# Reordering the start of a fused attention and long-convolution kernel: two head groups per key tile, taps spread by TensorE, x turned in the background, three load buffers

## The chip, the cores and the metric

The kernel runs on one core of a Trainium2 chip. The metric is device time in microseconds (us), the median of several runs. Engine names in the profile: PE is TensorE (PEld its weight loads), DVE is VectorE, ACT is ScalarE, POOL is GpSimd, SP is the engine whose queue issues most loads. A name such as L423 is a line of that kernel's source; a "q" behind an engine's name is its queue for issuing transfers.

## The reference, cut to what matters

```python
# A: attention, S=2048, D=512, 32 heads of 16
qkv = (x @ wqkv).reshape(B, S, 3, H, Dh).transpose(2, 0, 3, 1, 4)
p = softmax(einsum("bhqd,bhkd->bhqk", q, k) * Dh ** -0.5)
a = einsum("bhqk,bhkd->bhqd", p, v).transpose(...).reshape(B, S, D) @ wo
# B: 4-tap shift, then a causal convolution as long as the sequence
k_shift = sum_t k_pad[:, t:t + S, :] * shift_k[:, 3 - t]
kv = k_shift * v
y = irfft(rfft(kv, 2S) * rfft(ssm_k, 2S))[:S] + kv * ssm_D
b = q * y
out = concatenate([a, b], -1)
```

## The kernel before

The program records operations per engine, and each engine works its own list in order (the stop before 73.16 us, below, shows one list holding up another for 4.11 us). The main loop runs over *chunks*: a chunk is two or three blocks, and a block is one head's scores of 128 keys against 512 queries, one bank of PSUM (the array PS, to which every matmul of the traces writes; exp reads 128x1536 f32 from it for three blocks; copying a result out of a bank is called *evacuating* it). Four heads are a group. Per chunk TensorE makes the scores, ScalarE takes one exp over all the chunk's banks, and two chunks later TensorE multiplies by V ("PV"). The *taps* are the four factors per channel of the shift in B; the *pieces* (key pieces and convolution pieces are the same thing) are the VectorE operations that make kv from k, v and the taps. In between comes one *background* slot: first the projection units of Q, K and V (`early`), later the convolution on TensorE, with further Q projections and the output projection at its boundaries.

```python
def emit_qk(T):                     # scores of chunk T, then exp
    ... e.matmul(PS[:, bank, :], lhsT=KTo[...], rhs=QT[...], tile_position=(32 * s, 0))
    h_exp[T] = act.op(lambda e: e.activation(PT[:, T % R_PT, 0:n * QB], PS[:, banks...], ACT.Exp, scale=SCALE), ...)

# the taps: 512 KB broadcast load, then one ScalarE copy that transposes them
h_tb[0] = act.op(lambda e: e.activation(TB.rearrange("p m d -> p d m"), TRAW, ACT.Copy), [h_traw])

def kv_chunk(j):                    # 256 keys: 8 "pieces" on VectorE
    b = kvbuf[j % 2]                # two load buffers: k shifted by 0..3, and v
    ... 4 multiplies by a tap, 3 adds, then two multiplies by v; then load_kv(j + 2)

early = [("v", 0), ("v", 1), ("v", 2), ("k", 0, 1), ("v", 3), ...]   # units, one a chunk
def emit_bg(T):                     # the background slot of chunk T
    if st["early"] < len(early):
        unit(early[st["early"]], (5, 7)[T % 2] ...)   # 4 matmuls, then VectorE evacuates
        return
    if not kv_pieces and not st["started"]:
        st["started"] = True
        load_wop(...); load_wr(d) for 12 convolution rows; load_qn(...)
    ... turn / output projection / later q units / conv_lags(...)

for T in range(NT + 3):
    emit_qk(T)
    ... PV of chunk T-2 ...
    emit_bg(T)
    for _ in range(1 if T < 20 else 2):
        if kv_pieces and T >= 1:
            kv_pieces.pop(0)()      # convolution pieces on VectorE
```

The convolution needs every piece: its right-hand rows (`WR`, 512 KB each, loaded with a skew from a scratch tensor) reuse the load buffers' memory, so they are asked for only after the last piece. Cuts are marked by dots.

The softmax here doesn't subtract the row's maximum and nothing guards it: scores larger than these inputs give would overflow.

## Time and profile before

| | before |
|---|---|
| time | 1025.4 us median (1025.0 to 1025.6) |
| span of the profiled run | 1023.0 us |
| ScalarE busy | 948.8 us, of which exp 933.3 |
| first exp starts | 21.8 us |
| chunk 56 starts | 134.9 us |
| last exp ends | 1008.2 us |

The profile's page, kernel before. First the busy time of each engine, then two rows of the timeline in 40 slices (each digit is the busy share of a slice in tenths), then the chain that ended last, by engine:

```profile
PE 764.5 (75%) x12876; PEld 344.8 (34%) x12876; DVE 312.7 (31%) x478; ACT 948.8 (93%) x701; POOL 57.6 (6%) x82
...
DVE  3789413232203232321122423122222231222222
ACT  7766589999999999999999899999999999999994
...
ACT 78%; PE 9%; DVE 6%; DMA 5%; POOL 1%; SPq 1%; issue 0%; ACTq 0%; DVEq 0%
```

ScalarE is the bound: it is at 9 from the seventh slice on but for one 8 and the last slice, and 78% of the chain. The large losses are where its digits are below 9, above all in the first 140 us. Here is the ScalarE timeline of the first stretch (start, duration, engine, line, operation, out<-in, shapes, how many merged; in brackets the idle time before it and who ended that). L423 is exp:

```profile
13.01 9.30 ACT L377 ACTIVATE WR<-WR 128x2048 bf16<-128x2048 bf16 x1 [0.19 <-DMA WR<-in_B_shift_k_dram]
21.82 4.02 ACT L423 ACTIVATE PT<-PS 128x1536 bf16<-128x1536 f32 x3
...
45.47 1.45 ACT L423 ACTIVATE PT<-PS 128x1536 bf16<-128x1536 f32 x1 [0.60 <-PE PS L416]
47.08 1.02 ACT L423 ACTIVATE PT<-PS 128x1024 bf16<-128x1024 f32 x1 [0.16 <-PE PS L416]
...
73.16 2.54 ACT L423 ACTIVATE PT<-PS 128x1024 bf16<-128x1024 f32 x2 [5.63 <-PE PS L416]
...
124.28 5.81 ACT L423 ACTIVATE PT<-PS 128x1536 bf16<-128x1536 f32 x4 [9.35 <-PE PS L416]
134.86 26.65 ACT L423 ACTIVATE PT<-PS 128x1536 bf16<-128x1536 f32 x19 [4.77 <-PE PS L416]
```

Four things are to be seen. ScalarE transposes the taps for 9.30 us before the first exp. From 27 to 55 us the exps are apart: 45.47 to 47.08 is 1.61 us for a chunk, while the exps alone last 1.45 and 1.02. There is a stop of 5.63 us before 73.16. And there are stops of 9.35 and 4.77 us before 124.28 and 134.86. Counting exps one by one gives the number of the chunk: chunk 56 is the one at 134.86, and the remaining 636 chunks have three banks each, except the last.

The windows view of the same kernel, a line for each stretch (busy us of each engine with the number of instructions, then the granted TensorE clock, the share of the 16 DMA engines, and GB/s):

```profile
core 0: us, PE busy (x) PEld busy (x) DVE busy (x) ACT busy (x) POOL busy (x), PEclk, DMA share, GB/s
60.00:80.00 20.00, 14.41 (x68) 3.87 (x68) 17.66 (x32) 11.41 (x11) 4.05 (x7) 0.83 0.60 219
80.00:100.00 20.00, 12.74 (x74) 3.91 (x74) 18.57 (x32) 11.72 (x10) 10.80 (x15) 1.00 0.56 180
```

From 60 to 100 us VectorE is 88 to 93% busy, ScalarE under 60%. The stop of 5.63 us before 73.16 shows how one list holds up another (a line of VectorE's timeline and one of TensorE's):

```profile
68.80 0.69 DVE L325 TENSOR_TENSOR WR<-WR 128x1024 bf16<-128x1024 bf16 x1 [2.05 <-DMA WR<-in_B_v_dram]
70.14 0.62 PE L449 MATMUL PS<-PT,VAF 128*32 128x512 bf16 x4 [4.11 <-DVE OF L464]
```

VectorE waits 2.05 us for a load; the copy that frees the bank of the first group's PV (L464) stands behind that in its list, and TensorE waits 4.11 us for the copy. And in TensorE's timeline the first convolution matmul waits for its rows:

```profile
123.04 0.66 PE L560 MATMUL PS<-WR,KV 128*16 128x128 bf16 x16 [8.85 <-DMA WR<-kz_scratch]
```

### The profile page before, as it was taken

The page shows a single profiled execution, that of the slowest core. Times are in us where ns is not written, and L with a number is a line of the kernel's source. Part 1 is how long each engine was busy: PE and PEld are TensorE (multiplying, and loading weights), DVE is VectorE, ACT ScalarE, POOL GpSimd, SP SyncE. Part 2 cuts the span into 40 slices and gives each one's busy share as a digit, 9 for nine tenths or more (in the row PEclk, how much of TensorE's full clock was granted, in tenths as well). Part 3 has the DMA queues.
Part 4 walks back from the last instruction along what each step waited for, and adds up shares of the span by engine and source line. Part 5 has one row for each costly group of instructions (what it writes and reads, how often), then busy time and mean ns, then how long its engine had stood idle before and what let it go on. Part 6 is the DMA issues. An engine that isn't in the chain of part 4 may idle for free.

```text
span 1023.0 us, 27854 instructions
## 1 busy us (share of the span) xinstructions
PE 764.5 (75%) x12876; PEld 344.8 (34%) x12876; DVE 312.7 (31%) x478; ACT 948.8 (93%) x701; POOL 57.6 (6%) x82
## 2 busy tenths in 40 slices
PE   6986667776778777777676967776777786768887
PEld 2322233333333333333333333333333333331111
DVE  3789413232203232321122423122222231222222
ACT  7766589999999999999999899999999999999994
POOL 4124300000001000000000000000000000000000
PEclk8989789999999999999999999999999999995557
DMA  9254699899997798999999498999999959950000
GB/s 319 83 190 154 168 392 401 301 366 353 366 391 271 264 389 299 369 331 379 385 379 405 162 335 329 359 343 376 390 383 373 395 195 385 377 187 9 1 1 21
DMA packets 85124, 296.07 MB, mean 289 GB/s; under 512 B 10768, under 2 KB 14865, under 8 KB 84624
## 3 DMA queue, kind: packets, MB, share of 16 engines
q1 hardware_dynamic: 77760, 275.94, 71.8%
q0 software_dynamic: 5232, 16.78, 5.4%
q8 instruction: 101, 1.65, 0.6%
q10 hardware_dynamic: 2016, 1.57, 0.5%
q14 instruction: 15, 0.12, 0.0%
HBM read 287.83 MB, written 6.42 MB: 288 GB/s over the span
## 4 chain that ended last, share of the span: by engine, by line
ACT 78%; PE 9%; DVE 6%; DMA 5%; POOL 1%; SPq 1%; issue 0%; ACTq 0%; DVEq 0%
ACT PT L423 77%; PE PS L512 3%; DMA WR<-kz_scratch 2%; PE PS L268 2%; PE PS L416 2%; PE PS L282 1%; PE PS L449 1%; DMA WR<-in_B_v_dram 1%; DVE QT L296 1%; DMA WR<-in_B_shift_k_dram 1%; DVE WR L325 1%; ACT WR L377 1%; DVE WR L329 1%; DVE OUTA L520 1%; DVE DN L472 1%; POOL WR L148 1%
## 5 line engine op out<-in xcount | busy, mean ns | idle before, releaser
L423 ACT ACTIVATE PT<-PS 128x1536 bf16<-128x1536 f32 (+1 forms) x692 | 933.3, 1668 | 53.1 <-PE PS L416 52.7
L416 PE MATMUL PS<-QT,KTo 32*128 32x512 bf16 x2048 | 287.5, 409 | 211.0 <-ACT PT L423 209.3
L560 PE MATMUL PS<-WR,KV 128*16 128x128 bf16 (+15 forms) x8192 | 304.9, 223 | 20.0 <-DMA WR<-kz_scratch 16.2
L449 PE MATMUL PS<-PT,VAF 128*32 128x512 bf16 x2048 | 292.6, 414 | 4.1 <-DVE OF L464 4.1
L560 PEld LDWEIGHTS PS<-WR,KV 128*14 128x14 bf16 (+15 forms) x8192 | 204.6, 106 | 42.3 <-issue 26.7
L416 PEld LDWEIGHTS PS<-QT,KTo 32*128 32x128 bf16 x2048 | 67.8, 91 | 375.3 <-ACT PT L423 341.7
L449 PEld LDWEIGHTS PS<-PT,VAF 128*32 128x32 bf16 x2048 | 69.2, 94 | 177.1 <-issue 165.8
L464 DVE COPY OF<-PS 128x512 f32<-128x512 f32 x32 | 22.1, 692 | 341.4 <-PE PS L449 341.4
L472 DVE RECIPROCAL DN<-DN 128x128 f32<-128x128 f32 x128 | 110.7, 916 | 0.9
L576 DVE CAST YB<-PS 128x512 bf16<-128x512 f32 x32 | 22.1, 691 | 274.5 <-PE PS L560 274.4
L148 POOL DMA_DIRECT2D out_dram<-QN x4 | 4.7, 1171 | 622.9 <-DVE QN L596 622.9
L268 PE MATMUL PS<-xT,WQP 128*128 128x512 bf16 x128 | 34.0, 389 | 6.2 <-DVE KTo L300 3.2
L512 PE MATMUL PS<-WKV,OTN 128*128 128x512 bf16 x128 | 34.5, 399 | 3.6 <-DVE OTN L477 2.3
L148 POOL DMA_DIRECT2D WR<-in_B_k_dram x35 | 24.7, 710 | 63.7 <-DVE KV L334 54.5
L296 DVE CAST QT<-PS 128x512 bf16<-128x512 f32 x32 | 22.0, 689 | 20.1 <-PE PS L268 20.1
L466 DVE STREAM_SHUFFLE DN<-OF 128x512 f32<-128x512 f32 x32 | 24.9, 777 | 0.0
L477 DVE TENSOR_TENSOR OTN<-OF,DN 128x512 bf16<-128x512 f32 (+1 forms) x35 | 23.3, 667 | 1.0
L275 PE MATMUL PS<-xT,WKV 128*128 128x512 bf16 x64 | 18.5, 416 | 5.5 <-DVE KTo L300 4.4
L325 DVE TENSOR_TENSOR WR<-WR 128x1024 bf16<-128x1024 bf16 x32 | 21.5, 677 | 3.2 <-DMA WR<-in_B_v_dram 3.2
L282 PE MATMUL PS<-WKV,xT 128*128 128x512 bf16 x64 | 18.8, 422 | 0.0
L512 PEld LDWEIGHTS PS<-WKV,OTN 128*128 128x128 bf16 x128 | 10.8, 101 | 21.8 <-issue 6.0
L268 PEld LDWEIGHTS PS<-xT,WQP 128*128 128x128 bf16 x128 | 10.1, 98 | 23.0 <-DVE QT L296 7.0
(45 smaller groups left out, 161.1 us busy)
## 6 DMA issues: line engine op xcount, KB each, us to landing
WR<-kz_scratch SPq DMA_DIRECT2D x512, 512.0 KB, 7.8
WR<-in_B_k_dram POOLq DMA_DIRECT2D x29, 256.0 KB, 3.7
kz_scratch<-WR SPq DMA_DIRECT2D x1, 2176.0 KB, 9.4
KV<-in_A_x_dram SPq DMA_DIRECT2D x4, 512.0 KB, 7.2
WR<-in_B_v_dram POOLq DMA_DIRECT2D x8, 256.0 KB, 4.5
QN<-in_B_q_dram POOLq DMA_DIRECT2D x4, 512.0 KB, 10.9
out_dram<-QN POOLq DMA_DIRECT2D x4, 512.0 KB, 8.0
out_dram<-OUTA POOLq DMA_DIRECT2D x12, 128.0 KB, 2.8
```

Source lines behind the costliest of these rows:

```text
L148: f(outp, inp).then_inc(dsem.sem, 16)
L268: return e.matmul(PS[:, bank, :], lhsT=WQP[:, dc, g, :], rhs=xT[:, dc, qb * 512:(qb + 1) * 512], start=(dc == 0), stop=(dc == 3))
L282: return e.matmul(PS[:, bank, :], lhsT=xT[:, dc, kt * 128:(kt + 1) * 128], rhs=WV[:, dc, :], start=(dc == 0), stop=(dc == 3))
L296: hh = dve.op(lambda e: e.tensor_copy(QT[:, qb % 2, g, :], PS[:, bank, :]), [h, h_kzt[0] if qb == 1 else None])
L325: st[m] = dve.op(lambda e: e.tensor_tensor(b[:, m, :, :], b[:, m, :, :], in1, ALU.mult), [h_kv[j], h_tb[0]])
L416: ins = e.matmul(PS[:, bank, :], lhsT=KTo[32 * s:32 * s + 32, g // 2, kt * 128:(kt + 1) * 128], rhs=QT[32 * s:32 * s + 32, qb % 2, g, :], ...
L423: h_exp[T] = act.op(lambda e: e.activation(PT[:, T % R_PT, 0:n * QB], PS[:, banks[0]:banks[0] + n, :].rearrange("p b f -> p (b f)"), ACT.E ...
L449: ins = e.matmul(PS[32 * s:32 * s + 32, PVB, :], lhsT=VAF[:, kt, h * VW:h * VW + 32], rhs=PT[:, Tc % R_PT, j * QB:(j + 1) * QB], start=(kt ...
L466: h_sh = dve.op(lambda e: e.stream_shuffle(out=DN[:, r, :], in_=OF[:, r, :], mask=[DH] * 32), [h_of, h_otn.get(n - 2)])
L472: rec[i] = dve.op(lambda e: e.reciprocal(DN[:, r, sl], DN[:, r, sl]), [h_sh])
L512: ins = e.matmul(PS[:, bank, :], lhsT=OTN[:, oslot(qb * NG + g), t * 128:(t + 1) * 128], rhs=WOP[:, g, :], start=(g == 0), stop=(g == NG - 1))
L560: ins = e.matmul(PS[32 * c:32 * c + NB - n, BGB, 128 * (kk % 4):128 * (kk % 4) + 128], lhsT=KV[:, n:NB, d], rhs=WR[:, d % R_W, 128 * (NB - ...
```

## The change

The intent is to feed ScalarE from the start. The first two head groups are worked together, so a K or V tile serves 8 blocks instead of 4 and fewer projection units are needed per chunk; the second group's PV gets its own bank (7). The taps are broadcast by TensorE, with no large load. Only half of x is turned (transposed) before the first chunk, the rest as background units. The key pieces start at chunk 8 at two a chunk, with three load buffers, v and one shifted copy of k issued from the SP queue, and key chunks taken from the last to the first. The convolution starts ten chunks after its rows could be asked for. Core of the diff, cuts marked by dots:

```diff
-N_EARLY = 52
+N_EARLY = 56
...
-    h_traw = dma(act, d_tap, TRAW, <broadcast of B_shift_k, 512 KB>)
+    h_shk = dma(act, d_tap, SHK[:, :, :], B_shift_k.rearrange("(c p) m -> p c m", p=128))
...
-        b = kvbuf[j % 2]
-        deps = [h_kvfree.get(j - 2), h_edge]
+        b = kvbuf[(7 - j) % 3]
+        deps = [h_kvfree.get(j + 3), h_edge]
+        if j == 0:
+            z = wr_flat[0:3, ...]
+            deps = [pool.op(lambda e: e.memset(z, 0.0), deps)]
...
+            q = sp if m == 3 else pool
...
+    kv_pieces += [kz_turn x 4] + [kz_store, lambda: load_kv(5, h_kzt[0])]
-    for j in range(8):
+    for j in range(7, -1, -1):
         kv_pieces += kv_chunk(j)
...
+    def taps(ms, banks):
+        ... e.matmul(PS[:, bank, ...], lhsT=SHK[:, c, m:m + 1].broadcast_to([128, 128]), rhs=IDN[:, :], ...)
+            h_tb[m] = bank_free[bank] = act.op(lambda e: e.activation(TB[:, m, :], PS[:, bank, :], ACT.Copy), [h])
...
     def blk(i):
         s = i % 4
+        if i < 8 * KT:
+            return 0, (i // 4) % 2, i // 8, s
...
+    def pvb(n):
+        return BGB if n == 1 else PVB
...
-    early = [("v", 0), ("v", 1), ("v", 2), ("k", 0, 1), ...
+    early = [("v", 0), ("v", 1), ("x", 2, 0), ("v", 2), ("x", 2, 1), ("k", 0, 1), ...
...
-            if st["early"] >= 20 and T % 3 == 2:
+            if T % 5 in (1, 3) and T >= 4:
                 return
-            unit(early[st["early"]], (5, 7)[T % 2] if T < N_EARLY - 2 else 7)
+            unit(early[st["early"]], 5 if T < N_EARLY - 1 else 7)
...
-            st["started"] = True
+            st["started"] = T + 10
...
-        for _ in range(1 if T < 20 else 2):
-            if kv_pieces and T >= 1:
+        for _ in range(1 if T < 3 else 0 if T < 8 else 2):
+            if kv_pieces:
```

More of the change, by code (lines that the diff above doesn't have):

```diff
@@ L122, in bass_concat_heads__mha_block__ssm_conv_h3__prompt_kernel @@
     IDN = sb("IDN", [128, 128])
+    SHK = sb("SHK", [128, 4, 4])
     JNK = sb("JNK", [128, 2], FP32)
@@ L131, in bass_concat_heads__mha_block__ssm_conv_h3__prompt_kernel @@
     o1 = 5 * S
-    kvbuf = [wr_flat[:, o1 + 5120 * i:o1 + 5120 * i + 5120].rearrange("p (m t d) -> p m t d", m=5, t=2)
-             for i in range(2)]
-    TRAW = wr_flat[:, o1 + 10240:o1 + 12288].rearrange("p (d m) -> p d m", m=4)
-    TB = wr_flat[:, o1 + 12288:o1 + 14336].rearrange("p (m d) -> p m d", m=4)
+    TB = wr_flat[:, o1 + 10240:o1 + 12288].rearrange("p (m d) -> p m d", m=4)
     KZN = [QT[:, 1, :, :].rearrange("p g f -> p (g f)").rearrange("p (c s) -> p c s", c=2),
            QN[:, :, :, :].rearrange("p b t d -> p (b t d)").rearrange("p (c s) -> p c s", c=2)]
+    kvbuf = [[wr_flat[:, o1 + 5120 * i + 1024 * m:o1 + 5120 * i + 1024 * m + 1024] for m in range(5)] for i in range(2)]
+    kvbuf.append([QT[:, 1, 2 * m:2 * m + 2, :].rearrange("p g f -> p (g f)") for m in range(4)]
+                 + [QN[:, 0, 0:8, :].rearrange("p t d -> p (t d)")])
+    kvbuf = [[a.rearrange("p (t d) -> p t d", t=2) for a in b] for b in kvbuf]
     PS = enter(nc.psum_tensor("PS", [128, 8, 512], FP32))
@@ L154, in bass_concat_heads__mha_block__ssm_conv_h3__prompt_kernel @@
     d_kv = [DmaSem(sem(f"d_kv{i}")) for i in range(8)]
+    d_kp = [DmaSem(sem(f"d_kp{i}")) for i in range(8)]
     d_tap, d_kz, d_kzw, d_wo = [DmaSem(sem(n)) for n in ("d_tap", "d_kz", "d_kzw", "d_wo")]
@@ L173, in bass_concat_heads__mha_block__ssm_conv_h3__prompt_kernel @@
     h_wv = dma(act, d_w[2], WV, wview[:, :, 2 * D:3 * D])
-    h_traw = dma(act, d_tap, TRAW, bass.AP(tensor=B_shift_k.tensor, offset=B_shift_k[0, 0].offset,
-                                          ap=[[0, 128], [4, C], [1, 4]]))
     load_x(2)
@@ L183, in bass_concat_heads__mha_block__ssm_conv_h3__prompt_kernel @@
     h_kzl = dma(sp, d_kz, DSS, B_ssm_D.rearrange("(p c m) -> p c m", c=4, m=1))
-    h_kv = [None] * 8
+    h_kv = {}
     h_kvfree = {}
     def load_kv(j, h_edge=None):
-        b = kvbuf[j % 2]
-        deps = [h_kvfree.get(j - 2), h_edge]
-        kap = k2[2 * j * 128:2 * j * 128 + 256, :].rearrange("(t p) d -> p t d", p=128)
-        vap = v2[2 * j * 128:2 * j * 128 + 256, :].rearrange("(t p) d -> p t d", p=128)
+        b = kvbuf[(7 - j) % 3]
+        deps = [h_kvfree.get(j + 3), h_edge]
+        if j == 0:
+            z = wr_flat[0:3, o1 + 5120 + 1024:o1 + 5120 + 4096]
+            deps = [pool.op(lambda e: e.memset(z, 0.0), deps)]
+        r0 = 2 * j * 128
+        dma(sp, d_kv[j], b[4], v2[r0:r0 + 256, :].rearrange("(t p) d -> p t d", p=128), deps)
         for m in range(4):
+            q = sp if m == 3 else pool
+            ds = d_kv[j] if m == 3 else d_kp[j]
             if j == 0 and m > 0:
-                dma(pool, d_kv[j], b[m:128, m, 0, :], k2[0:128 - m, :], deps)
-                src = bass.AP(tensor=kap.tensor, offset=k2[128 - m, 0].offset, ap=[[D, 128], [1, D]])
-                dma(pool, d_kv[j], b[:, m, 1, :], src, deps)
-            else:
-                src = bass.AP(tensor=kap.tensor, offset=k2[2 * j * 128 - m, 0].offset,
-                              ap=[[D, 128], [128 * D, 2], [1, D]])
-                dma(pool, d_kv[j], b[:, m, :, :], src, deps)
-        h_kv[j] = dma(pool, d_kv[j], b[:, 4, :, :], vap, deps)
+                h = dma(q, ds, b[m][m:128, 0, :], k2[0:128 - m, :], deps)
+                src = bass.AP(tensor=k2.tensor, offset=k2[128 - m, 0].offset, ap=[[D, 128], [1, D]])
+                h = dma(q, ds, b[m][:, 1, :], src, deps)
+            else:
+                src = bass.AP(tensor=k2.tensor, offset=k2[r0 - m, 0].offset, ap=[[D, 128], [128 * D, 2], [1, D]])
+                h = dma(q, ds, b[m], src, deps)
+            if m >= 2:
+                h_kv[(j, m - 2)] = h
     h_j = dve.op(lambda e: e.memset(JNK[:], 0.0))
@@ L214, in bass_concat_heads__mha_block__ssm_conv_h3__prompt_kernel @@
     h_vaf1 = pool.op(lambda e: e.memset(VAF[:, :, H * VW:VROW], 1.0))
-    h_kvz = pool.op(lambda e: e.memset(kvbuf[0][0:3, 1:4, 0, :], 0.0))
     h_kz0 = pool.op(lambda e: e.memset(KZS[:, :, S:S + PAD], 0.0))
     pool.op(lambda e: e.wait_ge(*h_xn[3]), inc=False)
-    load_kv(0, h_kvz)
-    load_kv(1)
+    load_kv(7, h_xn[3])
+    load_kv(6, h_xn[3])
     act.op(lambda e: e.activation(JNK[:, 1:2], JNK[:, 0:1], ACT.Exp), [h_j], inc=False)
@@ L235, in bass_concat_heads__mha_block__ssm_conv_h3__prompt_kernel, with turn_x, fn @@
     h_x = {}
-    def turn_x(sc, b0, engs):
-        h_x[sc] = []
-        for cp in range(2):
-            pbf = PS[:, b0 + cp, :].bitcast(BF16)
-            def fn(e, cp=cp, pbf=pbf):
-                ins = None
-                for i in range(2):
-                    for t in range(4):
-                        c = 2 * cp + i
-                        ins = e.transpose(pbf[:, 512 * i + 128 * t:512 * i + 128 * t + 128],
-                                          KV[:, 4 * sc + t, 128 * c:128 * c + 128], IDN[:, :])
-                return ins
-            h = pe.op(fn, [h_xn[sc], h_idn, bank_free[b0 + cp]])
-            dst = xT[:, 2 * cp:2 * cp + 2, sc * 512:(sc + 1) * 512]
-            src = pbf.rearrange("p (i s) -> p i s", i=2)
-            if engs[cp] is act:
-                hh = act.op(lambda e, dst=dst, src=src: e.activation(dst, src, ACT.Copy), [h])
-            else:
-                hh = dve.op(lambda e, dst=dst, src=src: e.tensor_copy(dst, src), [h])
-            bank_free[b0 + cp] = hh
-            h_x[sc].append(hh)
+    h_xt = [None]
+    def turn_x(sc, cp, bank, eng):
+        pbf = PS[:, bank, :].bitcast(BF16)
+        def fn(e):
+            ins = None
+            for i in range(2):
+                for t in range(4):
+                    c = 2 * cp + i
+                    ins = e.transpose(pbf[:, 512 * i + 128 * t:512 * i + 128 * t + 128],
+                                      KV[:, 4 * sc + t, 128 * c:128 * c + 128], IDN[:, :])
+            return ins
+        h = pe.op(fn, [h_xn[sc], h_idn, bank_free[bank]])
+        h_xt[0] = h
+        dst = xT[:, 2 * cp:2 * cp + 2, sc * 512:(sc + 1) * 512]
+        src = pbf.rearrange("p (i s) -> p i s", i=2)
+        if eng is act:
+            hh = act.op(lambda e: e.activation(dst, src, ACT.Copy), [h])
+        else:
+            hh = dve.op(lambda e: e.tensor_copy(dst, src), [h])
+        bank_free[bank] = hh
+        h_x.setdefault(sc, []).append(hh)
     def pe_unit(u, bank):
@@ L310, in unit @@
     def unit(u, bank):
+        if u[0] == "x":
+            turn_x(u[1], u[2], bank, dve)
+            return
         evac_unit(u, bank, pe_unit(u, bank))
@@ L315, in bass_concat_heads__mha_block__ssm_conv_h3__prompt_kernel @@
     h_kvc = [None]
-    h_xt = [None]
-    h_tb = [None]
+    h_tb = {}
     def kv_chunk(j):
-        b = kvbuf[j % 2]
+        b = kvbuf[(7 - j) % 3]
         st = {}
@@ L324, in tap @@
             in1 = TB[:, m:m + 1, :].broadcast_to([128, 2, D])
-            st[m] = dve.op(lambda e: e.tensor_tensor(b[:, m, :, :], b[:, m, :, :], in1, ALU.mult),
-                           [h_kv[j], h_tb[0]])
+            st[m] = dve.op(lambda e: e.tensor_tensor(b[m], b[m], in1, ALU.mult),
+                           [h_kv[(j, 0)], h_kv[(j, 1)], h_tb[m]])
         def add(m):
-            st["a"] = dve.op(lambda e: e.tensor_tensor(b[:, 3, :, :], b[:, 3, :, :], b[:, m, :, :], ALU.add),
-                             [st[m], st[3], st.get("a")])
+            st["a"] = dve.op(lambda e: e.tensor_tensor(b[3], b[3], b[m], ALU.add), [st[m], st[3], st.get("a")])
         def last():
+            h = None
             for i in range(2):
-                h = dve.op(lambda e, i=i: e.tensor_tensor(KV[:, NB - 1 - 2 * j - i, :], b[:, 3, i, :], b[:, 4, i, :],
+                h = dve.op(lambda e, i=i: e.tensor_tensor(KV[:, NB - 1 - 2 * j - i, :], b[3][:, i, :], b[4][:, i, :],
                                                           ALU.mult), [st["a"], h_xt[0]])
@@ L337, in last @@
             h_kvc[0] = h
-            if j + 2 < 8:
-                load_kv(j + 2)
-        ps = [lambda m=m: tap(m) for m in (3, 2)] + [lambda: add(2), lambda: tap(1), lambda: add(1),
-                                                      lambda: tap(0), lambda: add(0), last]
-        return ps
+            if j >= 3:
+                load_kv(j - 3)
+        return [lambda m=m: tap(m) for m in (3, 2)] + [lambda: add(2), lambda: tap(1), lambda: add(1),
+                                                       lambda: tap(0), lambda: add(0), last]
     h_kzw = [None]
@@ L358, in bass_concat_heads__mha_block__ssm_conv_h3__prompt_kernel, with fn @@
         kv_pieces.append(lambda o=o: emit_wqp(o))
-    for j in range(8):
+    kv_pieces += [lambda c=c: kz_turn(c) for c in range(4)] + [kz_store, lambda: load_kv(5, h_kzt[0])]
+    for j in range(7, -1, -1):
         kv_pieces += kv_chunk(j)
-        if j == 1:
-            kv_pieces += [lambda c=c: kz_turn(c) for c in range(4)] + [kz_store]
+    def taps(ms, banks):
+        for m, bank in zip(ms, banks):
+            def fn(e, m=m, bank=bank):
+                ins = None
+                for c in range(4):
+                    ins = e.matmul(PS[:, bank, 128 * c:128 * c + 128],
+                                   lhsT=SHK[:, c, m:m + 1].broadcast_to([128, 128]), rhs=IDN[:, :],
+                                   start=(c == 0), stop=(c == 3))
+                return ins
+            h = pe.op(fn, [h_shk, h_idn, bank_free[bank]])
+            h_tb[m] = bank_free[bank] = act.op(
+                lambda e, m=m, bank=bank: e.activation(TB[:, m, :], PS[:, bank, :], ACT.Copy), [h])
     def warm(e):
@@ L371, in bass_concat_heads__mha_block__ssm_conv_h3__prompt_kernel @@
     emit_wqp(0)
-    turn_x(0, 0, (dve, act))
-    turn_x(1, 2, (dve, act))
+    turn_x(0, 0, 0, dve)
+    turn_x(0, 1, 1, act)
+    turn_x(1, 0, 2, dve)
+    turn_x(1, 1, 3, act)
+    taps((0, 1), (4, 5))
     unit(("q", 0, 0), 6)
     unit(("k", 0, 0), 7)
-    turn_x(2, 4, (act, act))
-    h_tb[0] = act.op(lambda e: e.activation(TB.rearrange("p m d -> p d m"), TRAW, ACT.Copy), [h_traw])
+    unit(("q", 0, 1), 6)
+    taps((2, 3), (4, 5))
     NBLK = NQB * NG * KT * 4
@@ L396, in blk @@
         return qb, g, kt, s
+    first, last_blk = {}, {}
+    for i in range(NBLK):
+        qb, g, kt, s = blk(i)
+        first.setdefault(qb * NG + g, i)
+        last_blk[qb * NG + g] = i
+    def pvb(n):
+        return BGB if n == 1 else PVB
     h_exp = {}
@@ L428, in emit_qk @@
             bank_free[bank] = h_exp[T]
-    h_pvb = [None]
     def oslot(n):
@@ L439, in emit_pv @@
         deps = [h_exp[chunk_of[b][0]] for b in bl] + [h_v[blk(b)[2]] for b in bl]
-        if any(blk(b)[2] == 0 for b in bl):
-            deps.append(h_pvb[0])
+        for b in bl:
+            qb, g, kt, s = blk(b)
+            if kt == 0:
+                deps.append(bank_free[pvb(qb * NG + g)])
         def fn(e):
@@ L448, in fn @@
                 Tc, j = chunk_of[b]
-                ins = e.matmul(PS[32 * s:32 * s + 32, PVB, :],
+                ins = e.matmul(PS[32 * s:32 * s + 32, pvb(qb * NG + g), :],
                                lhsT=VAF[:, kt, h * VW:h * VW + 32],
@@ L456, in emit_pv @@
             h_ptfree[chunk_of[b][0]] = h
-        if bl[-1] % (4 * KT) == 4 * KT - 1:
-            finish_group(bl[-1] // (4 * KT), h, T)
+        for b in bl:
+            qb, g, kt, s = blk(b)
+            if b == last_blk[qb * NG + g]:
+                finish_group(qb * NG + g, h, T)
     def finish_group(n, h, T):
@@ L463, in finish_group @@
         last = n == NQB * NG - 1
-        h_of = dve.op(lambda e: e.tensor_copy(OF[:, r, :], PS[:, PVB, :]), [h, h_otn.get(n - 2)])
-        h_pvb[0] = h_of
-        h_sh = dve.op(lambda e: e.stream_shuffle(out=DN[:, r, :], in_=OF[:, r, :], mask=[DH] * 32),
+        src = PS[:, pvb(n), :] if last else OF[:, r, :]
+        h_of = h
+        if not last:
+            h_of = dve.op(lambda e: e.tensor_copy(src, PS[:, pvb(n), :]), [h, h_otn.get(n - 2)])
+            bank_free[pvb(n)] = h_of
+        h_sh = dve.op(lambda e: e.stream_shuffle(out=DN[:, r, :], in_=src, mask=[DH] * 32),
                       [h_of, h_otn.get(n - 2)])
@@ L476, in mult @@
             h_otn[(n, i1)] = h_otn[n] = dve.op(
-                lambda e: e.tensor_tensor(OTN[:, oslot(n), sl], OF[:, r, sl], DN[:, r, sl], ALU.mult),
+                lambda e: e.tensor_tensor(OTN[:, oslot(n), sl], src[:, sl], DN[:, r, sl], ALU.mult),
                 [rec[i1 - 1], h_wqp[7]] + ([h_op[((n - R_O) // NG, t)] for t in range(4)] if n >= R_O else []))
@@ L602, in conv_turn @@
                 load_qn(sl + 2, [ho])
-    early = [("v", 0), ("v", 1), ("v", 2), ("k", 0, 1), ("v", 3), ("v", 4), ("v", 5), ("v", 6), ("k", 0, 2),
-             ("v", 7), ("v", 8), ("v", 9), ("v", 10), ("k", 0, 3), ("v", 11), ("v", 12), ("v", 13), ("v", 14),
-             ("v", 15), ("q", 0, 1)]
+    early = [("v", 0), ("v", 1), ("x", 2, 0), ("v", 2), ("x", 2, 1), ("k", 0, 1), ("v", 3), ("v", 4), ("x", 3, 0),
+             ("v", 5), ("x", 3, 1), ("v", 6), ("k", 0, 2), ("v", 7), ("v", 8), ("v", 9), ("v", 10), ("k", 0, 3),
+             ("v", 11), ("v", 12), ("v", 13), ("v", 14), ("v", 15)]
     for o in range(1, 4):
-        early += [("k", o, sc) for sc in range(4)] + [("q", 0, 2 * o), ("q", 0, 2 * o + 1)]
+        early += [("k", o, 0), ("q", 0, 2 * o)] + [("k", o, sc) for sc in range(1, 4)] + [("q", 0, 2 * o + 1)]
     later_q = [("q", qb, g) for qb in range(1, NQB) for g in range(NG)]
@@ L639, in emit_bg @@
             return
-        if st["qd"] % 8 == 0 and st["lag"] == 0:
+        if st["started"] and st["qd"] % 8 == 0 and st["lag"] == 0:
             if st["op"] < len(later_op):
@@ L647, in emit_bg @@
                     return
-            if st["gap"] < 3 and st["q"] < len(later_q):
+            if (st["gap"] < 3 or T < st["started"]) and st["q"] < len(later_q):
                 u = later_q[st["q"]]
@@ L654, in emit_bg @@
                     return
-        if st["started"] and st["qd"] < C // 4:
+        if st["started"] and T >= st["started"] and st["qd"] < C // 4:
             n0 = st["lag"]
@@ L669, in bass_concat_heads__mha_block__ssm_conv_h3__prompt_kernel @@
     for b in range(NBLK):
-        T = chunk_of[b][0]
-        t = T + 2
-        first = b - b % (4 * KT)
-        if b >= 4 * KT and chunk_of[first - 1][0] + 2 >= t:
-            t = chunk_of[first - 1][0] + 3
+        qb, g, kt, s = blk(b)
+        n = qb * NG + g
+        t = chunk_of[b][0] + 2
+        if n >= 2:
+            t = max(t, chunk_of[last_blk[n - 1]][0] + 3)
         pv_at.setdefault(t, []).append(b)
@@ L679, in bass_concat_heads__mha_block__ssm_conv_h3__prompt_kernel @@
             emit_qk(T)
-        if T == 0:
-            turn_x(3, 6, (dve, dve))
-            h_xt[0] = pe_last()
         if T == NT:
@@ L687, in bass_concat_heads__mha_block__ssm_conv_h3__prompt_kernel @@
         while pvs:
-            g0 = pvs[0] // (4 * KT)
-            now = [b for b in pvs if b // (4 * KT) == g0][:4]
-            pvs = [b for b in pvs if b not in now]
-            emit_pv(now, T)
+            emit_pv(pvs[:4], T)
+            pvs = pvs[4:]
         emit_bg(T)
```

## The prediction

> **What bounds the kernel now.** ScalarE's exponentials: the table of engines has ScalarE busy 949 of 1023 us (TensorE 765, VectorE 313); the exp line is 77% of the chain of waits. In the tail a 3-bank exp leaves every 1.34 us, so 692 chunks (666 of three banks, 26 of two) need about 915 us. The rest is starved ScalarE, by the timeline mostly before 135 us:
>
> - 0 to 22 us: first exp at 21.8; ScalarE waits for the broadcast tap load, then transposes taps for 9.30 us.
> - 27 to 55 us: every chunk carries a projection unit (4 matmuls, 0.97 us); TensorE sets 1.62 us a chunk where exp needs about 1.2.
> - 55 to 112 us: 1.9 us a chunk. VectorE is 88 to 93% busy from 60 to 100 us (taps, adds, evacuations in one queue), with stops for key loads; ScalarE idles up to 5.6 us at a time.
> - 114 to 135 us: 9.35 + 4.77 us idle; TensorE waits in order for the first convolution rows.
>
> Chunk 56 starts at 134.9 us. The other 636 take 872.6 us (1.37 each), the end 15.5 us.
>
> **What the change does.**
> 1. TensorE broadcasts the taps (16 small matmuls); four ScalarE copies of about 0.6 us replace the 9.30 us and a 512 KB load. First exp at 12.5 to 14 us: 8 to 9 us gained, on the critical path.
> 2. Each key tile feeds 8 blocks, so three units per five chunks suffice. TensorE: (5 x 0.65 + 3 x 0.97)/5 = 1.23 us a chunk, level with exp.
> 3. VectorE's work is not less. From chunk 8 to 43 it gets two convolution pieces a chunk: in the timeline the 8 pieces of a key chunk take 5.25 us; with 2.4 evacuations of 0.6 us per 4 chunks that is 1.67 us a chunk. Units share one bank, so TensorE follows. Three buffers and a second load queue should remove the load stops. So VectorE sets this stretch: chunk 8 at about 25 us (the ssm kernel rows land then), chunk 43 at 84 to 88, chunk 56 at about 103.
> 4. Convolution rows load once the last key chunk is done (about 87 us) while other chunks and query units go on; the convolution starts near chunk 77 (about 130 us). The 14 us stop vanishes.
> 5. From chunk 56 on: the same 636 chunks; six early units and some query units now fall there (about +3 us); the last group skips one 0.7 us copy. Row loads (2 MB per 4 chunks at about 400 GB/s) stay just within the 5.4 us that exp takes.
>
> Chunk 56 comes about 32 us earlier: 1025.4 - 32 + 3 - 0.7, about 995 us.
>
> **Right or wrong in the profile:** first exp at 12.5 to 14 us; no 9 us activation; VectorE over 90% busy from 30 to 85 us, chunk spacing near 1.7 us; no ScalarE gap over 4 us after 30 us; chunk 56 near 103 us; convolution first near chunk 77 without DMA wait; spacing later unchanged.
>
> **What would make it wrong:** kernel-row or key loads landing late and stopping VectorE's queue (up to 10 us slower); [...] TensorE running further ahead than I think, so that exp sets the pace (chunk 56 near 85 us, about 977 in all); convolution loads falling behind after the later start, or new stalls in the steady part.
>
> Time 995 us, range 983 to 1006. Faster by over 2%: 0.87; within 2%: 0.12; slower: 0.01.

The "about 400 GB/s" of the row loads is what the kernel before moves in its steady part: 391, 406 and 404 GB/s at a DMA share of 1.01 to 1.02 (windows 500 to 505, 505 to 510 and 600 to 605 us). The 0.6 us for a copy of a tap was my estimate; in the changed kernel four take 2.17 us.

## The result, and the profile after

The changed kernel took 992.9 us (991.1 to 993.7, 4 runs) against 1025.4 us: a ratio of 0.968, 95% interval 0.967 to 0.970. Ratios are the mean time of one kernel's fast runs over that of the other's of the same rounds, so not quite the ratio of the medians quoted. The prediction said 995 us.

The same parts of the page, changed kernel:

```profile
PE 750.7 (76%) x12892; PEld 346.0 (35%) x12892; DVE 311.5 (31%) x479; ACT 938.0 (95%) x702; POOL 46.6 (5%) x65
...
DVE  4997532221223321122232132322123322112222
ACT  5877899999999999999999999999999999999995
...
ACT 79%; DVE 10%; PE 9%; DMA 1%; issue 1%; ACTq 0%; DVEq 0%
```

The ScalarE timeline, changed kernel (L456 is exp, L381 the taps' copies):

```profile
12.64 1.09 ACT L381 ACTIVATE WR<-PS 128x512 bf16<-128x512 f32 x2 [2.32 <-PE PS L375]
13.61 2.59 ACT L456 ACTIVATE PT<-PS 128x1536 bf16<-128x1536 f32 x2
...
23.54 11.55 ACT L456 ACTIVATE PT<-PS 128x1536 bf16<-128x1536 f32 x10 [0.81 <-PE PS L449]
37.60 2.36 ACT L456 ACTIVATE PT<-PS 128x1536 bf16<-128x1536 f32 x2 [2.51 <-PE PS L449]
...
98.72 2.79 ACT L456 ACTIVATE PT<-PS 128x1536 bf16<-128x1536 f32 x2 [0.60 <-PE PS L449]
```

The taps take two copies here, 1.09 us together, and two earlier; the first exp starts at 13.61 instead of 21.82. Ten exps follow one another from 23.54 with no idle time. From 37.60 on there are stops of up to 2.5 us. Chunk 56 starts at 98.72 instead of 134.86. The windows view shows who sets the pace in between:

```profile
40.00:60.00 20.00, 15.62 (x95) 4.68 (x94) 19.76 (x36) 15.05 (x13) 6.48 (x9) 1.00 0.74 248
60.00:80.00 20.00, 15.30 (x91) 4.72 (x92) 19.79 (x36) 13.47 (x13) 5.58 (x6) 1.00 0.33 102
```

VectorE is 99% busy. It was the busiest engine of the corresponding stretch before too, at 88 to 93%; now it has hardly a pause left, and it is the bound (p1_one tests this). The convolution starts in chunk 75 without a wait for its rows (TensorE's timeline; L274 is a query unit, L449 the scores, L598 the convolution; the line has no bracket, so no idle time):

```profile
126.72 1.04 PE L274 MATMUL PS<-xT,WQP 128*128 128x512 bf16 x4
127.69 0.39 PE L449 MATMUL PS<-QT,KTo 32*128 32x512 bf16 x3
...
128.67 0.61 PE L598 MATMUL PS<-WR,KV 128*16 128x128 bf16 x16
```

From chunk 56 to the end of the last exp the changed kernel takes 877.5 us, the kernel before 873.3. So 36.1 us are gained by chunk 56, 4.1 (before rounding) given back, and the end after the last exp is 1.7 us shorter: 33.7 us, as the spans differ.

### The profile page after: what moved, and what is told of

Same layout as the page of the kernel before. It is cut to its first block, busy times and chain, and to the rows that moved or that the text cites. A ratio compares the mean times of both kernels' runs of the same rounds, so it can differ in the third digit from the quotient of the medians.

```text
span 989.3 us, 27897 instructions
## 1 busy us (share of the span) xinstructions
PE 750.7 (76%) x12892; PEld 346.0 (35%) x12892; DVE 311.5 (31%) x479; ACT 938.0 (95%) x702; POOL 46.6 (5%) x65
## 3 DMA queue, kind: packets, MB, share of 16 engines
q10 hardware_dynamic: 2400, 1.05, 0.4%
## 4 chain that ended last, share of the span: by engine, by line
ACT 79%; DVE 10%; PE 9%; DMA 1%; issue 1%; ACTq 0%; DVEq 0%
ACT PT L456 79%; PE PS L550 3%; PE PS L274 2%; DVE WR L333 1%; DVE QT L302 1%; PE PS L449 1%; DVE DN L510 1%; DVE WR L337 1%; PE PS L482 1%; DVE VAF L312 1%; DMA WKV<-in_A_wqkv_dram 1%; PE PS L281 1%; DVE OUTA L558 1%; DVE KTo L306 1%; PE PS L288 1%
## 5 line engine op out<-in xcount | busy, mean ns | idle before, releaser
L456 ACT ACTIVATE PT<-PS 128x1536 bf16<-128x1536 f32 (+1 forms) x692 | 931.3, 1644 | 31.2 <-PE PS L449 31.1
L449 PE MATMUL PS<-QT,KTo 32*128 32x512 bf16 x2048 | 282.9, 402 | 204.8 <-ACT PT L456 203.6
L598 PE MATMUL PS<-WR,KV 128*15 128x128 bf16 (+15 forms) x8192 | 306.0, 223 | 3.7 <-DVE QN L634 1.5
L482 PE MATMUL PS<-PT,VAF 128*32 128x512 bf16 x2048 | 288.2, 407 | 0.0
L598 PEld LDWEIGHTS PS<-WR,KV 128*6 128x6 bf16 (+15 forms) x8192 | 206.1, 106 | 23.8 <-issue 8.5
L449 PEld LDWEIGHTS PS<-QT,KTo 32*128 32x128 bf16 x2048 | 67.6, 91 | 360.9 <-ACT PT L456 328.1
L150 POOL DMA_DIRECT2D out_dram<-QN x4 | 4.7, 1168 | 695.2 <-DVE QN L634 695.2
L274 PE MATMUL PS<-xT,WQP 128*128 128x512 bf16 x128 | 33.2, 382 | 5.4 <-DVE KTo L306 2.2
L515 DVE TENSOR_TENSOR OTN<-OF,DN 128x512 bf16<-128x512 f32 x31 | 22.1, 713 | 0.8
L288 PE MATMUL PS<-WKV,xT 128*128 128x512 bf16 x64 | 17.2, 393 | 6.6 <-DVE VAF L312 4.4
L558 DVE CAST OUTA<-PS 128x512 bf16<-128x512 f32 x12 | 8.3, 691 | 32.4 <-PE PS L550 32.4
L274 PEld LDWEIGHTS PS<-xT,WQP 128*128 128x128 bf16 x128 | 10.0, 98 | 22.0 <-DVE QT L302 7.5
L333 DVE TENSOR_TENSOR WR<-WR 128x1024 bf16<-128x1024 bf16 x24 | 15.9, 682 | 0.0
```

The source lines that it names most:

```text
L274: return e.matmul(PS[:, bank, :], lhsT=WQP[:, dc, g, :], rhs=xT[:, dc, qb * 512:(qb + 1) * 512], start=(dc == 0), stop=(dc == 3))
L288: return e.matmul(PS[:, bank, :], lhsT=xT[:, dc, kt * 128:(kt + 1) * 128], rhs=WV[:, dc, :], start=(dc == 0), stop=(dc == 3))
L333: st[m] = dve.op(lambda e: e.tensor_tensor(b[m], b[m], in1, ALU.mult), [h_kv[(j, 0)], h_kv[(j, 1)], h_tb[m]])
L449: ins = e.matmul(PS[:, bank, :], lhsT=KTo[32 * s:32 * s + 32, g // 2, kt * 128:(kt + 1) * 128], rhs=QT[32 * s:32 * s + 32, qb % 2, g, :], ...
L482: ins = e.matmul(PS[32 * s:32 * s + 32, pvb(qb * NG + g), :], lhsT=VAF[:, kt, h * VW:h * VW + 32], rhs=PT[:, Tc % R_PT, j * QB:(j + 1) * Q ...
L598: ins = e.matmul(PS[32 * c:32 * c + NB - n, BGB, 128 * (kk % 4):128 * (kk % 4) + 128], lhsT=KV[:, n:NB, d], rhs=WR[:, d % R_W, 128 * (NB - ...
```

## The experiments

Twelve kernels ran, all with correct results, each timed in 3 rounds against the kernel before on the same chip. On those chips the kernel before had medians of 1024.0 to 1026.0 us, so differences of 1 us between rows of different chips mean nothing. The first column of times is the median, the ratio is to the kernel before. Chunk times are starts of exps, counted in each trace.

| kernel | us | ratio | first exp | chunk 43 | chunk 56 | 56 to last exp's end |
|---|---|---|---|---|---|---|
| before | 1025.4 | 1 | 21.8 | 100.9 | 134.9 | 873.3 |
| changed | 992.9 | 0.968 | 13.6 | 80.9 | 98.7 | 877.5 |
| u1_traw | 1000.6 | 0.976 | 22.0 | 90.2 | 108.0 | 877.5 |
| u2_twobuf | 998.3 | 0.974 | 13.4 | 87.3 | 104.5 | 878.2 |
| u3_start0 | 993.0 | 0.968 | 13.4 | 82.7 | 100.5 | 877.8 |
| u4_nointer | 1003.3 | 0.978 | 14.9 | 91.3 | 113.3 | 874.1 |
| u4_nointer_start0 | 1010.6 | 0.987 | 14.9 | 92.0 | 116.9 | 878.6 |
| u5_poolq | 992.3 | 0.969 | 13.1 | 82.1 | 99.9 | 877.1 |
| u6_xfront | 997.2 | 0.973 | 14.7 | 86.7 | 104.4 | 878.1 |
| b1_taps | 1019.1 | 0.993 | 15.8 | 92.8 | 127.3 | 874.8 |
| p1_one | 990.2 | 0.966 | 13.4 | 69.2 | 89.0 | 886.3 |
| p2_onehalf | 988.8 | 0.965 | 13.3 | 72.8 | 94.6 | 880.0 |
| c1_space | 979.8 | 0.955 | 13.4 | 82.1 | 99.3 | 864.7 |
| c2_space_spread | 975.1 | 0.951 | 13.1 | 72.6 | 91.1 | 868.2 |

My theory was the prediction's: four separate causes of starvation in the first 135 us, with VectorE as the bound that remains. The rivals put the gain on one part (the interleaving, or the second load queue, or the convolution's delay), or had parts absorbed by what follows.

### The taps: u1_traw and b1_taps

```diff
-    taps((0, 1), (4, 5))
...
-    taps((2, 3), (4, 5))
+    h_t = act.op(lambda e: e.activation(TB.rearrange("p m d -> p d m"), TRAW, ACT.Copy), [h_traw])
```

(with the old broadcast load and buffer back in place)

> Undoes only the taps (broadcast load and one ScalarE transposing copy, as before). My theory: the 9.3 us copy again lies in front of the first exp and VectorE's bound stretch only starts after it, so everything shifts: first exp at 21 to 23 us (13.6 in the changed kernel), chunk 56 at 105 to 108 us (98.7), total +7 to +9 us, about 1001 us. Rival: VectorE sets the pace afterwards and would use the time, so most of it is absorbed: less than +3 us.

1000.6 us, 7.7 more than the changed kernel. The ScalarE timeline of u1_traw:

```profile
13.23 9.30 ACT L400 ACTIVATE WR<-WR 128x2048 bf16<-128x2048 bf16 x1 [3.83 <-DMA WR<-in_B_shift_k_dram]
22.03 4.01 ACT L459 ACTIVATE PT<-PS 128x1536 bf16<-128x1536 f32 x3
```

The first exp is 8.4 us later, chunk 56 is 9.3 us later: nothing is absorbed by then. The rival falls.

The reverse, this part alone in the kernel before (the `taps` function, the small load, and the two calls in place of the old copy):

> The kernel before with one part of the change alone: taps spread by TensorE. My theory: the 8 to 9 us in front of the first exp are saved here too, but the stretch behind it meets the key loads and the convolution rows at the same place, so nearly all of the shift arrives at the end: first exp at 13 to 14 us, total -6 to -9 us against before, about 1017 us. Rival: the loads that follow do not move, so most is given back: less than -3 us.

1019.1 us, 6.9 less than the kernel before on the same chip (1026.0). The first exp came at 15.8 us, not at 13 to 14 as I expected, since this kernel still turns the third quarter of x on ScalarE (two copies from 11.77 to 13.71) before it. The saving arrives at the end almost whole. The two stops at the convolution's start are still there (ScalarE waits 9.97 and 4.29 us for scores before 117.21 and 127.33 us), although the pieces end 7.7 us earlier: that alone does not remove the stop.

### The third load buffer: u2_twobuf

```diff
-        b = kvbuf[(7 - j) % 3]
-        deps = [h_kvfree.get(j + 3), h_edge]
+        b = kvbuf[(7 - j) % 2]
+        deps = [h_kvfree.get(j + 2), h_edge]
...
-            if j >= 3:
-                load_kv(j - 3)
+            if j >= 2:
+                load_kv(j - 2)
```

> Undoes only the third load buffer (loads for a key chunk start when the chunk two before it is done). My theory: loads take 5 to 9.5 us to land and one key chunk takes VectorE 6.6 us, so with only one chunk of lead VectorE stops 1 to 3 us in most of six chunks: +6 to +12 us, about 1001 us, VectorE waiting for the loads in the trace. Rival: the loads land in time (second queue is enough): less than +1 us.

998.3 us, 5.4 more. The sum is just under the range, but my reason was wrong. VectorE waits for a load once, not in six chunks. VectorE's timeline (L342 ends a key chunk, L333 begins the next):

```profile
76.97 0.76 DVE L342 TENSOR_TENSOR KV<-WR 128x512 bf16<-128x512 bf16 x2
80.75 0.69 DVE L333 TENSOR_TENSOR WR<-WR 128x1024 bf16<-128x1024 bf16 x1 [3.02 <-DMA WR<-in_B_k_dram]
```

And GpSimd's queue ahead of that, where L195 zeroes the edge and L150 issues the loads:

```profile
71.22 2.65 POOL L195 MEMSET WR<- 3x3072 bf16 x1 [4.06 <-DVE KV L342]
74.16 2.93 POOL L150 DMA_DIRECT2D WR<-in_B_k_dram  x5 [0.30 <-POOL WR L195]
```

Only the last key chunk worked, the one that holds the start of the sequence, comes late. Its buffer must first be zeroed at the edge (2.65 us on GpSimd), and then its loads are issued; VectorE stops for 3.02 us, and ScalarE, behind TensorE behind VectorE, for 6.05. The other key chunks land in time with two buffers. The third buffer hides the edge chunk, nothing else. In the kernel before, the edge chunk is worked first, and its buffer is zeroed before anything is loaded (1.37 us from 2.62 us on), so there this stop does not exist. The third buffer thus makes good what the reversed order of the key chunks costs; its 5.4 us are no gain over the kernel before. Two buffers with the old order were not tried in the changed kernel.

### The second load queue: u5_poolq

```diff
-        dma(sp, d_kv[j], b[4], ...
+        dma(pool, d_kv[j], b[4], ...
...
-            q = sp if m == 3 else pool
+            q = pool
```

> Undoes only the second load queue: all five loads of a key chunk issued by GpSimd. My theory: five issues of 0.71 us are 3.6 us, below the 6.6 us that VectorE takes for a key chunk, and three buffers give two chunks of lead, so VectorE does not wait except perhaps for the first key chunk: 0 to +2 us, about 994 us. Rival: GpSimd's queue was what stopped VectorE before: +4 us or more.

992.3 us against 992.9: no difference. With three buffers the second queue is worth nothing; with two buffers it was not tried, and there one may stand in for the other. Nor did it cost anything that GpSimd issued all 5 loads of a key chunk beside a busy VectorE: VectorE was 95% busy from 30 to 80 us (47.56 of 50), and the time did not move.

### Turning x in the background: u6_xfront

```diff
     turn_x(1, 1, 3, act)
+    turn_x(2, 0, 0, dve)
+    turn_x(2, 1, 1, act)
...
+        if T == 0:
+            turn_x(3, 0, 6, dve)
+            turn_x(3, 1, 5, dve)
```

(and the four `("x", ...)` units taken out of `early`)

> Undoes only the turning of x as background units: the third quarter of x is turned before the first chunk, the fourth right after the first chunk's scores. My theory: the first exp comes 1 to 1.5 us later, and the following stretch is set by VectorE, whose work is the same: -1 to +2 us, about 994 us. Rival: keeping x out of the start is worth 4 us or more.

997.2 us, 4.3 more: the rival is right here (the intervals of the two ratios, 0.970 to 0.976 and 0.967 to 0.970, just touch, so the size is rough). The first exp is only 1.1 us later, but chunk 3 starts at 21.4 instead of 18.5 us. TensorE's timeline shows why (L252 turns x, L288 is a V unit, L451 the scores):

```profile
14.39 1.15 PE L252 MATMUL PS<-IDN,KV 128*128 128x128 bf16 x16
16.38 1.04 PE L288 MATMUL PS<-WKV,xT 128*128 128x512 bf16 x4 [0.84 <-DVE xT L262]
17.35 0.39 PE L451 MATMUL PS<-QT,KTo 32*128 32x512 bf16 x2
```

The 16 transposes of the last quarter stand between the scores of chunk 0 and the V unit, the unit then waits 0.84 us for the evacuation of x by VectorE, and the scores of chunk 1 come only at 17.35 (14.75 in the changed kernel). Before VectorE is loaded, the time of each chunk is TensorE's list, and work moved there is paid at once.

### Interleaving two head groups: u4_nointer

```diff
-        if i < 8 * KT:
-            return 0, (i // 4) % 2, i // 8, s
...
-        return BGB if n == 1 else PVB
+        return PVB
...
     (the old list of units, the first 20 in every slot, and two banks in turn for them;
      x turned in front as in u6_xfront; the extra query unit before chunk 0 removed)
```

> Undoes only the interleaving of the first two groups (one unit in every one of the first 20 chunks, x turned in front, old list of units). My theory: VectorE is the bound from chunk 8, so the interleaving is worth little there: chunks 8 to 20 cost 1.9 us instead of 1.5, the first exp comes 1 to 2 us later: +4 to +8 us, about 998 us. Rival: the interleaving is the main gain: +15 us or more.

1003.3 us, 10.4 more: over my range, short of the rival's. It is not a clean undoing: one unit in every slot leaves no room for x, which had to be turned in front, and the units have two banks again. u6_xfront put a price of 4.3 us on turning x in front, so about 6 us remain for the interleaving and the banks (a difference of two runs, an estimate).

### The convolution's delay: u3_start0 and u4_nointer_start0

```diff
-            st["started"] = T + 10
+            st["started"] = T
```

> Undoes only the ten chunks of delay before the convolution. My theory: the first rows had landed at about 101 us and the early units keep the convolution away until about chunk 67 (113 us) anyway, so the delay does nothing: within 1 us of the changed kernel (993). Rival: the delay is what removed the 14 us stop: TensorE waits for convolution rows again, +5 us or more.

993.0 us: no difference. Yet the stop of 14 us is gone in this kernel. The reason I had written down was that the early units keep the convolution away until the rows are there (they end at chunk 64 in fact). The first convolution matmul of u3_start0 waits for no row (two short waits, 0.84 and 1.89 us, come later):

```profile
121.32 0.47 PE L598 MATMUL PS<-WR,KV 128*16 128x128 bf16 x16 [0.23 <-DVE QT L302]
```

To test that reason, the same edit was made in u4_nointer, where the early units end near chunk 47:

> As u4_nointer (first two groups not interleaved, so the early units end near chunk 47) and also without the ten chunks of delay of the convolution. My theory: the delay did nothing in u3_start0 only because the early units kept the convolution away until the rows were there; here rows are asked for at 94 us and the convolution would start near 103 us, about 9 us after, where before it took 13 us from asking to the first convolution matmul: TensorE waits 3 us or more for convolution rows, total +1 to +5 us over u4_nointer (1003), about 1006 us. Rival: the delay does nothing here either, because VectorE's earlier end alone removed the stop: within 1 us of u4_nointer, no wait for rows.

1010.6 us, 7.3 more than u4_nointer. TensorE's timeline of u4_nointer_start0, the first matmuls of the first three groups of rows:

```profile
105.17 0.46 PE L597 MATMUL PS<-WR,KV 128*16 128x128 bf16 x16 [0.28 <-DVE QT L302]
...
115.68 0.66 PE L597 MATMUL PS<-WR,KV 128*16 128x128 bf16 x16 [6.47 <-DMA WR<-kz_scratch]
...
125.41 0.66 PE L597 MATMUL PS<-WR,KV 128*16 128x128 bf16 x16 [4.22 <-DMA WR<-kz_scratch]
```

The first four rows were there, the next two groups were not: 6.47 and 4.22 us of waiting, more than I expected. In u4_nointer, with the delay, the first matmul has no wait:

```profile
113.80 0.61 PE L597 MATMUL PS<-WR,KV 128*16 128x128 bf16 x16
```

So time between the end of the key pieces and the convolution is what removes the stop. In the changed kernel both the delay and the longer early list give it, and either alone is enough; with neither, the stop is back.

Why do the rows take so long? Twelve rows of 512 KB are asked for at once, 6.3 MB: even at the 414 GB/s below that is 15 us (an estimate from these two numbers), and TensorE cannot begin without the first four. In the kernel before they also came more slowly than that. There, right after the rows were asked for, the DMA engines were full while moving little:

```profile
115.00:120.00 5.00, 0.00 (x0) 0.00 (x0) 0.00 (x0) 0.00 (x0) 3.18 (x4) 0.70 1.04 267
120.00:125.00 5.00, 1.96 (x38) 1.22 (x38) 0.17 (x1) 0.72 (x1) 0.00 (x0) 0.50 1.04 225
```

In the changed kernel, as long after its rows were asked for (at 84 us there, at 110 before), the same share moved more:

```profile
88.00:93.00 5.00, 4.86 (x32) 1.51 (x30) 2.26 (x4) 4.64 (x5) 0.00 (x0) 1.00 1.00 384
93.00:98.00 5.00, 4.45 (x26) 1.39 (x24) 4.95 (x9) 4.49 (x4) 0.00 (x0) 1.00 1.02 414
```

In the kernel before and in u4_nointer_start0 the loads of q and of the output weights run in the same microseconds; in the changed kernel they wait for the end of the early list and come after 116 us, when the rows have landed. The rates differ with them: 225 to 267 GB/s at a share of 1.04 in the kernel before, 414 at 1.02 in the changed one. The trace of u4_nointer_start0 narrows it down: the output weights were issued from 102.86 us on and the loads of q from 106.93 on, and the windows before and after that are

```profile
100.00:105.00 5.00, 4.62 (x25) 1.29 (x23) 2.08 (x3) 3.83 (x4) 4.71 (x6) 1.00 1.02 404
110.00:115.00 5.00, 0.00 (x0) 0.00 (x0) 1.93 (x3) 0.63 (x1) 0.00 (x0) 0.82 1.05 211
```

No run leaves these loads out, so that they slow the rows is argued from their timing, not shown by an experiment; nor is it shown how they would.

### VectorE as the bound: p1_one and p2_onehalf

```diff
-        for _ in range(1 if T < 3 else 0 if T < 8 else 2):
+        for _ in range(1 if T < 3 else 0 if T < 8 else 1):          # p1_one
+        for _ in range(1 if T < 3 else 0 if T < 8 else 1 + T % 2):  # p2_onehalf
```

> Changed kernel with one convolution piece per chunk instead of two from chunk 8 on, the work itself unchanged; the pieces end at chunk 77 instead of 43. My theory: VectorE's rate sets chunks 8 to 43 (1.57 us a chunk); with one piece it needs about 1.0 us a chunk and exp or TensorE sets about 1.25: chunk 56 at 84 to 88 us (98.8), convolution rows load from about 118 us and the convolution starts at chunk 88 with a wait of at most a few us: total -8 to -14 us, about 981 us. Rival: TensorE's in-order queue (projection units on one bank) sets that stretch: chunk 56 moves less than 4 us, total within 4 us.

990.2 us, 2.7 less; the intervals of the ratios overlap (0.964 to 0.969, and 0.967 to 0.970), so of the total only that it gained little is sure. The mechanism was right and the total wrong. Chunks 8 to 43 took 43.6 us instead of 55.1, that is 1.25 a chunk as expected, and chunk 56 came 9.7 us earlier; so VectorE had set the pace, not TensorE's list. But from chunk 56 on 8.8 us were given back. The windows view of p1_one:

```profile
30.00:69.00 39.00, 37.47 (x231) 11.89 (x232) 31.00 (x53) 35.91 (x32) 8.64 (x12) 1.00 0.54 193
69.00:90.00 21.00, 18.64 (x105) 5.44 (x105) 18.89 (x33) 16.16 (x15) 3.90 (x4) 0.92 0.18 64
90.00:111.00 21.00, 14.28 (x82) 3.89 (x83) 17.19 (x28) 14.58 (x12) 3.84 (x6) 0.84 0.21 63
```

Up to 69 us VectorE is 79% busy and TensorE 96%. Then the pieces still to do meet the reciprocals and shuffles of the first two groups, which end together at chunk 53, and VectorE is 90% busy from 69 to 90 and 82% to 111 with ScalarE at 77 and 69%. The convolution, later by then, also waited 3.1 us for its rows. How the 8.8 us divide between the two was not tested. Here the work moved off the bound came back where the same engine was next wanted.

> Changed kernel with one and two convolution pieces in turn (1.5 a chunk). My theory: VectorE needs 1.5 x 0.665 + 0.6 x 0.6 = 1.36 us a chunk: chunk 56 at 91 to 94 us, pieces end near chunk 55, no wait for rows: total -5 to -7 us, about 987 us, half of the way to one piece. Rival: within 2 us of the changed kernel.

988.8 us, 4.1 less, a little under the range expected, for the same reason: chunk 56 came 4.1 us earlier (I expected 5 to 8), and 2.5 us of the time after it were lost.

### A version that beats both: c1_space and c2_space_spread

In the steady part the profile of both kernels shows chunks of 1.6 to 1.8 us where a query or output unit stands in the background slot. ScalarE's timeline of the changed kernel, in such a bunch:

```profile
324.33 1.45 ACT L456 ACTIVATE PT<-PS 128x1536 bf16<-128x1536 f32 x1 [0.37 <-PE PS L449]
325.95 1.45 ACT L456 ACTIVATE PT<-PS 128x1536 bf16<-128x1536 f32 x1 [0.17 <-PE PS L449]
```

TensorE needs 0.39 + 0.39 + 0.97 us there, in order, while exp takes 1.34. With a unit only in every second chunk, the next chunk makes up for it: two chunks then take TensorE 4 x 0.39 + 0.97 = 2.53 us, below the 2.68 of two exps (an estimate from these times). The convolution of the changed kernel ends some 47 chunks early, so there are free slots:

```diff
+        if st["skip"]:
+            st["skip"] = False
+            return
...
             op_out(qb, t, BGB, op_mm(qb, t, 4, 8, BGB))
             st["half"] = None
+            st["skip"] = t < 3
...
                     st["half"] = (qb, t)
+                    st["skip"] = True
...
                     st["q"] += 1
+                    st["skip"] = st["gap"] < 3 or T < st["started"]
```

> Changed kernel, with one empty background slot between consecutive query or output-projection units after the early list (about 40 slots; the convolution now ends about 12 chunks before the end instead of 47). My theory: a chunk with such a unit needs 0.39 + 0.39 + 0.97 us of TensorE in order, more than exp's 1.34, and the trace shows 1.82 (query) and 1.72 us (output) a chunk in bunches; with a unit in every second chunk only, TensorE has its work done before exp needs it: about 20 x 0.48 + 21 x 0.38 = 17 us saved, about 976 us. Rival: the extra time of these bunches is the bank wait on VectorE's evacuation or it comes back at the end of the convolution: less than 4 us saved.

979.8 us, 13.1 less than the changed kernel, where 17 were expected; why it fell short was not looked into. The gain is where it should be: 864.7 us instead of 877.5 from chunk 56 on, and the rival falls. ScalarE's timeline of c1_space around its first output bunch:

```profile
289.23 61.45 ACT L456 ACTIVATE PT<-PS 128x1536 bf16<-128x1536 f32 x45
```

45 exps without a gap, where the changed kernel had one before each exp of its bunch. After chunk 56 ScalarE waits 2.8 us in all before exps, against 11.9 in the changed kernel.

The last kernel adds p2's spreading with a pause at chunks 50 to 59:

```diff
-        for _ in range(1 if T < 3 else 0 if T < 8 else 2):
+        for _ in range(1 if T < 3 else 0 if T < 8 else 1 + T % 2 if T < 50 else 0 if T < 60 else 1):
```

> As c1, and the convolution pieces at 1.5 a chunk from chunk 8 to 49, none from 50 to 59 (where the first two groups finish), then one a chunk. My theory: p2 lost part of its gain because pieces met the eight reciprocals at chunks 53 to 58; without that meeting the spreading gives -5 to -8 us on top of c1, about 970 us. Rival: no more than p2's 4 us, or less, as the pieces left over delay the rows.

975.1 us, 4.7 less than c1_space, at the low end of the range and hardly more than p2's 4.1. Chunk 56 comes at 91.1 (94.6 in p2), so the pause works, but pieces end later and TensorE waits 5.4 us in all for rows; 868.2 us from chunk 56 on, 3.5 more than c1. This is the fastest kernel: 4.9% under the kernel before.

## Why the prediction was right, point by point

1. *What bounds it, and that the starvation lies mostly before 135 us*: right, and so did the gain of this change: by chunk 56 36.1 us (predicted 32), and 4.1 given back later (predicted 3). But there were 13 us to be had after it, in the bunches of units, which the prediction passed over (c1_space).
2. *Taps, first exp at 12.5 to 14 us, 8 to 9 us gained*: right. 13.6 us; undoing it cost 7.7 us.
3. *VectorE sets chunks 8 to 43 at 1.67 us each; chunk 43 at 84 to 88, chunk 56 at 103*: the mechanism was right (VectorE 99% busy, p1_one), chunk 56 came 4 us sooner. Chunks 20 to 43 took 1.66 us each (38.1 us for 23), but 8 to 20 only 1.41. I let VectorE rule from chunk 8 on; in fact TensorE and ScalarE kept going while VectorE's backlog built up, with the first stop of over 1 us (2.51) at chunk 16.
4. *"Three buffers and a second load queue should remove the load stops"*: the stops were gone, but they had been 3.2 us in all, and the reasons are half wrong. With three buffers the second queue did nothing (u5_poolq); with two queues the third buffer hid only the edge chunk, which the new order puts last (u2_twobuf). Both undone at once was not tried.
5. *The convolution near chunk 77, the 14 us stop gone*: right (chunk 75, 128.7 us, no wait). The prediction let the rows load from 87 us on and the convolution start at about 130, without saying which part of the change makes that room. Room is what counts (u4_nointer_start0); the longer early list or the delay alone gives enough of it (u3_start0, u4_nointer), and an earlier end of the pieces alone does not (b1_taps).
6. *What I left out*: turning x in the background is worth 4.3 us (u6_xfront), as much as some parts that I costed.

Added up, the parts undone one after another cost 7.7 (taps), 5.4 (third buffer), 10.4 (interleaving together with x) and 7.3 (room before the convolution): 30.8 of the 32.5 us. Undoings need not add, and the third buffer's 5.4 us undo a cost that the new order itself brings, so this is a rough check of size and no split. The reversed order, the new schedule of the pieces and the copy left out at the end were not undone by themselves.

## What to carry to other kernels

When one engine starves another through a chain of in-order lists, find the engine that is busy in that very stretch, and expect work taken out of it to return at the next place where it is wanted: p1_one kept about 2 of 9.7 us (2.7 by the medians, 1.7 by the profiled spans). A load that is needed at once after a late release wants other work between the release and its first use, and here it did not matter which of two kinds of work that was. And where a background unit makes a chunk longer than the bound's own step, place such units in every second step: this was worth 13 us here, more than any single part of the change.

## What else the traces show

- The granted clock at the end. In the changed kernel the granted TensorE clock falls to 0.50 at about 912.9 us (1.00 from 911 to 912, 0.93 from 912 to 913, 0.50 from 913 to 914), 5.6 us after the last convolution matmul (907.3), and stays there for over 50 us (915 to 973 us). TensorE is never idle for more than 0.63 us at a time from 904 us to the fall, and mostly for 0.19 us after it. The windows view, and a line of TensorE's timeline in that stretch:

```profile
940.00:960.00 20.00, 17.33 (x90) 3.15 (x90) 5.50 (x8) 20.00 (x16) 0.00 (x0) 0.50 0.00 1
```

```profile
935.93 0.61 PE L449 MATMUL PS<-QT,KTo 32*128 32x512 bf16 x3 [0.19 <-ACT PT L456]
```

  Three scores' matmuls take 0.61 us here and 0.39 in the part before; with two such groups in every 1.34 us TensorE is idle for 0.19. What brings the clock down is not shown: with the convolution, matmul work went from 0.39 + 0.40 + 0.61 us a chunk to 0.39 + 0.40, and the kind of matmul changed too. In c1_space, whose convolution runs nearly to the end, the granted clock from 900 to 960 us is 0.93 against 0.61 here. It costs nothing in this kernel, as ScalarE is 100% busy in the stretch in both. (Matmul ends are modelled in the profile, so the busy share itself is rough.)
- The loads beside the convolution rows. With the loads of q and of the output weights beside them, the DMA engines moved 225 GB/s in all at a share of 1.04 in the kernel before, and in u4_nointer_start0 404 at 1.02 before the loads of q began and 211 at 1.05 after; where the rows ran alone, in the changed kernel, it was 414 at 1.02. That the loads of q are the cause was not isolated.
- Memsets on GpSimd: 3 partitions of 3072 bf16 elements took 2.65 us, which was the start of u2_twobuf's stop, and 128 partitions of 4096 took 3.51 us in the kernel before. Both are 0.86 ns for each element of one partition, so between these two the number of partitions made no difference.
